# Values of three pairs loaded through GpSimd's casting queue, a last store on ScalarE's queue, zero matmuls in 16 places, and a new order of issue, in a gated recurrence with a two-layer feed-forward on one core

## The chip, the core and the metric

The kernel runs on one core of one Trainium2 chip. The time is device microseconds of one execution. The kernel before was timed five times: the median is 197.15 us, the lowest 194.38 us, the highest 199.48 us. One further execution was profiled; its own time was 197.51 us.

## The reference

There are 4 batches, 8 heads, 768 tokens and 48 numbers per head. For each batch and head a 48 x 48 state runs along the tokens, and its output goes through a two-layer network with the smooth activation 0.5 (h + sqrt(h^2 + 4)):

```
f = 1 / (1 + exp(-f_logit))
for t in range(768):
    state = f[t][:, None] * state + k[t][:, None] * v[t][None, :]
    y[t] = q[t] @ state
x = y as (4 * 768, 8 * 48)
h = x @ w_in                       # 384 x 2048
out = (0.5 * (h + sqrt(h * h + 4))) @ w_out   # 2048 x 384
```

All inputs and the output are float32 in device memory; the kernel multiplies in fp16 and accumulates in float32.

## The kernel before, in words

The tokens are cut into 12 pairs of chunks, 256 tokens each, three pairs to a batch. Token 2u+i of a pair lies on partition u, so that one partition's row of one head is two neighbouring tokens, 384 bytes in memory. Pair 0 is cut in two halves of four heads (FINE, line 18), the others are whole.

Each pair passes through these pieces, and their names are the words that the order is written in (the number after the name is the pair):

- lf, lk, lq, lv (lines 169 to 177): the loads of the gate, the keys, the queries and the values, 384 KB each, issued by SyncE.
- ex, ut, tt, ln, hi, lo (lines 179 to 268): the logarithm of the gates, split into two fp16 parts. ex and ln are ScalarE, ut is VectorE, the others can be on several engines.
- cu (line 272): TensorE sums the logarithms along the tokens. For pairs 0 to 2 it fills two banks, for the later ones one bank, and c1 (line 299) makes the second sum on VectorE.
- ep, ea (line 308) and ge (line 350): exponentials of the sums on ScalarE. gs and gb (lines 356 and 363) make decay factors of them.
- qu, ku (lines 320 and 326) and qm, km (line 333): queries and keys are scaled by the gates, into fp16 (the tile qk).
- vc (line 340): the values are cast to fp16 by a copy on VectorE, GpSimd or ScalarE.
- tp and te: for pairs 0 to 3 the scaled queries and keys are transposed by TensorE (line 381) and copied out (line 395). tx (line 371): for pairs 4 to 11 a transposing DMA issued by SyncE does it.
- sc (line 406) and pm (line 427): scores inside a chunk and their mask. kv (line 435): keys times values. sa, sb, sp, ia: the state is carried from chunk to chunk. yt and yn (lines 484 and 499): the output of the recurrence; yc (line 506) copies it out.
- xp and xe (lines 522 and 529), or for pairs 4 to 11 the transposing DMA xx (line 514): the output is transposed for the network.
- m1 (line 537): eight pieces of six matmuls for the first layer. sq (line 547) squares, rt (line 554) takes the root, gt (line 563) finishes the activation on VectorE. m2 (line 574): the second layer in two halves of four pieces. ev (line 585) copies the result out, st (line 595) stores it.
- wi and wo (lines 147 and 152): the weights, loaded and cast to fp16 by DMAs that GpSimd issues.

What runs when is one list, ORDER (lines 31 to 105), written ahead by a planner from the costs and the sets of reads and uses that stand beside each piece. A word is a name, a colon, the engine (D VectorE, P GpSimd, A ScalarE, S SyncE, T TensorE) and, for TensorE, an @ with the PSUM banks that the piece starts to use. The loop at line 685 emits the words in this order. So each engine has its own queue, in the order of its words in the list, and runs it strictly in turn; a word that waits for another engine holds up everything behind it on its own engine. A word that takes a buffer or a bank waits until the readers of what stood there are done (DEPTH, line 29, says how many buffers a name has; `os`, the tile that ev fills and st stores, has 2). TABLE:e and TABLE:s load one of two tables of functions into ScalarE.

The code already knows words that begin with wm (line 693): n matmuls of the identity into a bank that nothing reads. The order before uses none.

## Time and profile before

| what | us |
|---|---|
| median of five executions (lowest to highest) | 197.15 (194.38 to 199.48) |
| the profiled execution, its own time | 197.51 |
| its span, first to last instruction of the program | 195.3 |
| TensorE busy with matmuls in the span | 171.4 |
| VectorE, ScalarE, GpSimd busy | 151.5, 153.6, 117.5 |
| start of the first matmul | 6.45 |
| start of the first matmuls of the first layer (line 541) | 22.32 |
| end of the last matmul | 190.9 |
| start of the last two stores' issue on SyncE | 191.45 and 192.05 |

The profile's page gives busy time by engine, and the span in 40 slices of 4.9 us. The timeline gives instructions in order of time, those of one line merged, with the idle time of the engine before them and what ended it in brackets. The table of stretches gives, for any stretch, each engine's busy time, the clock that TensorE was granted, and what the DMA engines moved. PEld is the load of a stationary operand, which overlaps the matmuls. Times are from the span's start.

### The profile page before, as it was taken

The page shows a single profiled execution, that of the slowest core. Times are in us where ns is not written, and L with a number is a line of the kernel's source. Part 1 is how long each engine was busy: PE and PEld are TensorE (multiplying, and loading weights), DVE is VectorE, ACT ScalarE, POOL GpSimd, SP SyncE. Part 2 cuts the span into 40 slices and gives each one's busy share as a digit, 9 for nine tenths or more (in the row PEclk, how much of TensorE's full clock was granted, in tenths as well). Part 3 has the DMA queues.
Part 4 walks back from the last instruction along what each step waited for, and adds up shares of the span by engine and source line. Part 5 has one row for each costly group of instructions (what it writes and reads, how often), then busy time and mean ns, then how long its engine had stood idle before and what let it go on. Part 6 is the DMA issues. An engine that isn't in the chain of part 4 may idle for free.

```text
span 195.3 us, 5596 instructions
## 1 busy us (share of the span) xinstructions
PE 171.4 (88%) x2287; PEld 124.1 (64%) x2287; DVE 151.5 (78%) x280; ACT 153.6 (79%) x246; POOL 117.5 (60%) x146
## 2 busy tenths in 40 slices
PE   0348993789999999899999999999969999999990
...
PEclk9999999699999999999999999999999999999999
...
GB/s 142 268 256 236 245 219 248 213 237 226 223 242 121 226 251 136 263 215 228 209 230 206 230 145 229 169 189 53 31 153 147 51 85 82 3 0 0 164 68 93
DMA packets 80505, 32.87 MB, mean 168 GB/s; under 512 B 73824, under 2 KB 80480, under 8 KB 80480
## 3 DMA queue, kind: packets, MB, share of 16 engines
q1 hardware_dynamic: 76768, 29.37, 74.4%
q0 software_dynamic: 3712, 3.15, 10.0%
...
## 4 chain that ended last, share of the span: by engine, by line
PE 45%; POOL 23%; DMA 13%; issue 8%; DVE 5%; ACT 3%; SPq 1%; POOLq 0%; DVEq 0%
PE ps L541 19%; PE ps L578 19%; POOL qk L142 7%; DMA qkT<-qk 5%; DMA f<-in_f_logit_dram 3%; POOL k L142 3%; DMA k<-in_k_dram 3%; POOL UT L142 3%; DMA xT<-y 3%; DVE qk L142 2%; POOL v L139 2%; POOL q L142 2%; PE ps L414 2%; PE ps L492 2%; POOL hl L266 1%
## 5 line engine op out<-in xcount | busy, mean ns | idle before, releaser
L541 PE MATMUL ps<-xT,win 128*128 128x256 f16 x576 | 73.7, 276 | 3.2 <-ACT os L137 1.4
L566 DVE SCALAR_TENSOR_TENSOR g<-ps,r 128x512 f16<-128x512 f32 x96 | 62.4, 684 | 17.4 <-ACT r L556 17.2
L578 PE MATMUL ps<-wout,g 128*128 128x384 f16 x384 | 71.2, 327 | 0.0
L550 ACT ACTIVATE hsq<-ps 128x512 f16<-128x512 f32 x96 | 54.0, 592 | 16.4 <-PE ps L541 15.8
L541 PEld LDWEIGHTS <-win 128*128 128x128 f16 x576 | 55.3, 99 | 15.0 <-issue 2.3
L556 ACT ACTIVATE r<-hsq 128x1024 f16<-128x1024 f16 x48 | 50.6, 1057 | 1.2
L578 PEld LDWEIGHTS <-g 128*128 128x128 f16 x384 | 36.1, 98 | 19.5
L429 DVE TENSOR_TENSOR pm<-ps,mask 128x512 f16<-128x512 f32 x48 | 30.9, 683 | 3.8 <-PE ps L414 3.7
L142 POOL TENSOR_TENSOR qk<-q,ea 128x384 f16<-128x384 f32 x22 | 22.2, 1031 | 1.3 <-DVE q L142 0.9
L142 POOL TENSOR_TENSOR k<-k,UT 128x768 f32<-128x768 f32 x9 | 16.3, 1811 | 4.1 <-DMA k<-in_k_dram 4.1
L142 POOL TENSOR_TENSOR qk<-k,ep 128x384 f16<-128x384 f32 x18 | 17.6, 998 | 0.1
L283 PE MATMUL ps<-hl,tri 128*128 128x384 f16 (+1 forms) x34 | 9.2, 377 | 9.1 <-ACT hl L258 6.5
L181 ACT ACTIVATE f<-f 128x768 f32<-128x768 f32 (+1 forms) x13 | 10.3, 792 | 4.2 <-DMA f<-in_f_logit_dram 4.0
L139 POOL CAST v<-v 128x768 f16<-128x768 f32 (+1 forms) x11 | 9.0, 822 | 6.3 <-DMA v<-in_v_dram 6.3
L142 POOL TENSOR_TENSOR UT<-UT 128x384 f32<-128x384 f32 (+1 forms) x9 | 9.1, 1012 | 4.4 <-DVE UT L231 4.4
L137 ACT COPY os<-ps 128x384 f32<-128x384 f32 x9 | 4.3, 480 | 8.8 <-PE ps L578 5.0
L142 POOL TENSOR_TENSOR q<-q,UT 128x384 f32<-128x384 f32 x9 | 9.0, 996 | 3.8 <-DMA q<-in_q_dram 3.8
L414 PE MATMUL ps<-qkT 48*64 48x128 f16 x384 | 9.7, 228 | 1.5 <-ACT qkT L137 0.6
L266 POOL TENSOR_TENSOR hl<-s,hl 128x384 f16<-128x384 f32 (+1 forms) x11 | 10.1, 915 | 0.8 <-ACT hl L258 0.7
L414 PEld LDWEIGHTS <-qkT 48*64 48x64 f16 x384 | 6.7, 110 | 5.7 <-issue 3.2
L139 DVE CAST y<-ps 128x384 f16<-128x384 f32 x17 | 9.3, 550 | 0.9 <-PE ps L501 0.9
L139 DVE COPY os<-ps 128x384 f32<-128x384 f32 x15 | 8.2, 548 | 2.1 <-PE ps L578 2.1
...
## 6 DMA issues: line engine op xcount, KB each, us to landing
...
```

Source lines behind the costliest of these rows:

```text
L139: eng(e).tensor_copy(out=o, in_=i)
L142: eng(e).tensor_tensor(out=o, in0=a, in1=b, op=ALU.mult)
L181: nc.scalar.activation(out=t, in_=t, func=AF.Exp, scale=-1.0)
L266: eng(e).tensor_tensor(out=hl[:, 1, hs, 0:D], in0=T["s", p][:, hs], in1=hl[:, 0, hs, 0:D], op=ALU.subtract)
L283: nc.tensor.matmul(out=T["cum", p, m][:, h0 * D:h1 * D], lhsT=tri[:, m], rhs=t[:, hs, 0:D], start=(r == 0), stop=(r == len(terms) - 1), sk ...
L414: nc.tensor.matmul(out=T["sc", p, i, h][64 * cc:64 * cc + 64, j, :], lhsT=t[r, 1, j, i, :], rhs=t[r, 0, j], start=True, stop=True)
L429: eng(e).tensor_tensor(out=T["pm", p, i, h], in0=T["pc", p, i, h] if key in PMACT else T["sc", p, i, h], in1=K["mask"][:, i].unsqueeze(1). ...
L541: nc.tensor.matmul(out=T["h", p, m][:, a], lhsT=K["win"][m // 2][:, j, m % 2 * 256 + a * 128:m % 2 * 256 + a * 128 + 128], rhs=T["xT", p][ ...
L550: nc.scalar.activation(out=T["hsq", p, r][:, a], in_=T["h", p, m].rearrange("p a c t -> p (a c t)"), func=AF.Square, scale=1.0)
L556: nc.scalar.activation(out=T["r16", p, r], in_=T["hsq", p, r], func=AF.Sqrt, scale=0.25, bias=1.0)
L566: nc.vector.scalar_tensor_tensor(out=T["g", p][:, 2 * m:2 * m + 2, :].rearrange("p a t -> p (a t)"), in0=T["h", p, m].rearrange("p a c t - ...
L578: nc.tensor.matmul(out=T["o", p, cc], lhsT=T["g", p][:, jn, cc * 128:(cc + 1) * 128], rhs=K["wout"][jn // 4][:, jn % 4, :], start=(jn == 0 ...
```

## The change

- **Values by GpSimd's queue.** For pairs 1, 2 and 3 the words lv and vc go. In their place vd is a DMA issued by GpSimd that reads the float32 values and writes the fp16 tile. vd1 stands behind gs0 and between wi0 and qu1 in GpSimd's queue, vd2 behind gb1, after wi3 and before gs2, vd3 between qu4 and ku4.
- **One last store by ScalarE.** Of the four stores of pair 11, st11.1.1 is issued by ScalarE, directly behind ev11.1 in its queue, and st11.1.0 stays with SyncE.
- **Zero matmuls.** A tile of zeros, warm, is set by VectorE ahead of all other constants. Sixteen words wm3_n emit three matmuls of it each, 128 x 128: ten words between cu0.0 and tp0.0, one ahead of and one behind tp0.1, one ahead of m1.0.0, one behind m1.0.1, and two after the last m2. The number behind the underscore only makes the word unique.
- **The order.** The whole list is new. 39 words that stay change their engine between VectorE, GpSimd and ScalarE (qu2 from GpSimd to VectorE, km2 from VectorE to GpSimd, qm1 from GpSimd to VectorE, vc0.0 from GpSimd to ScalarE among them). The planner's cost of a store's issue by SyncE changes from 0.5 to 0.6.

The diff, with the list cut to what is spoken of:

```diff
@@ -27,81 +27,83 @@
+VDMA = [1, 2, 3]
...
-lf0.1:S lf0.0:S lf1.0:S lk0.0:S lk0.1:S TABLE:e ex0.1:A lq0.1:S ut0.1:D ex0.0:A lq0.0:S tt0.1:P ut0.0:D ln0.1:A tt0.0:D
-hi0.1:A ln0.0:A lf2.0:S lo0.1:P hi0.0:A ex1.0:A lo0.0:D lv0.0:S cu0.0:T@01 ku0.0:D ut1.0:D cu0.1:T@01 lk1.0:S ku0.1:D tt1.0:D
-ep0.1:A qu0.1:D ln1.0:A km0.1:D ea0.1:A ep0.0:A lq1.0:S qm0.1:D ea0.0:A hi1.0:A qu0.0:D tp0.1:T@12 lf3.0:S km0.0:D ex2.0:A
-qm0.0:D ge0:A te0.0.1:A ut2.0:D gs0:P lv0.1:S tp0.0:T@12 tt2.0:D lo1.0:P te0.0.0:A te0.1.0:D ln2.0:A lf4.0:S te0.1.1:D hi2.0:A
-ku1.0:D sc0.0:T@01 wi0:P sc0.1:T@23 cu1.0:T@45 wi2:P lv1.0:S qu1.0:D ex3.0:A pm0.01:D lk2.0:S lo2.0:P ea1.0:A pm0.10:D vc0.1:A
-vc0.0:P cu2.0:T@15 pm0.00:D lq2.0:S ge1:A qm1.0:P ep1.0:A pm0.11:D kv0:T@02 ge2:A ex4.0:A yt0:T@34 sa0:D km1.0:D yn0.1:T
-yc0.0:A gb1:P ia0.1:T yc0.1:A xp0.0:T@0 xe0.0:A xp0.1:T@3 ut3.0:D tp1.0:T@46 wi1:P xe0.1:A sb0:D ep2.0:A m1.0.1:T@0 tt3.0:P
-ea2.0:A te1.1.0:D m1.0.0:T@7 sq0.1:A wi3:P te1.0.0:D ln3.0:A lf5.0:S ut4.0:D sc1.0:T@12 gs1:P sq0.0:A sc1.1:T@34 pm1.00:D
-m1.0.4:T@5 TABLE:s rt0.0:A vc1.0:P pm1.11:D m1.0.5:T@1 tt4.0:P pm1.01:D kv1:T@46 gs2:P ia1.0:T pm1.10:D gb2:P hi3.0:P sq0.5:A
-lv2.0:S gt0.0:D yt1:T@23 ku2.0:P sq0.4:A yn1.0:T sa1:D m1.0.3:T@7 rt0.2:A yc1.0:D ia1.1:T m1.0.2:T@4 gt0.1:D sq0.3:A lo3.0:P
-yn1.1:T sb1:D xp1.0:T@0 sq0.2:A km2.0:D wo1:P rt0.1:A cu3.0:T@2 lk3.0:S m1.0.6:T@6 qu2.0:P yc1.1:D TABLE:e ln4.0:A c13.0:D
-xp1.1:T@3 lq4.0:S qm2.0:P xe1.1:D xe1.0:D m1.0.7:T@3 gt0.5:D ex5.0:A m1.1.1:T@0 gt0.2:D lq3.0:S ea3.0:A vc2.0:P gt0.4:D
-tp2.0:T@14 ge3:A sq0.7:A wo0:P ut5.0:D m1.1.3:T@5 sq1.1:A te2.1.0:D tt5.0:P sq0.6:A te2.0.0:D ep3.0:A wo2:P ln5.0:A lk4.0:S
...
-m2.7.00:T@0 gt7.5:D sq8.1:A st5.01.1:S m2.7.01:T gt7.6:D sq8.0:A tx10.1:S gs10:P m2.7.02:T gs11:P gt7.7:D rt8.0:A gb11:P
...
-m1.11.6:T@5 gt11.2:D m2.10.13:T sq11.6:A gt11.5:D m2.10.01:T sq11.7:A ev10.1:D m2.10.02:T rt11.3:A m2.11.01:T gt11.7:D
-m2.10.03:T gt11.6:D m2.11.02:T ev10.0:D m2.11.10:T@5 st10.01.1:S m2.11.11:T st10.01.0:S m2.11.03:T m2.11.12:T ev11.0:D
-m2.11.13:T st11.0.0:S st11.0.1:S ev11.1:A st11.1.0:S st11.1.1:S
...
+lf0.0:S lf0.1:S lf1.0:S lk0.0:S lk0.1:S TABLE:e ex0.0:A lq0.1:S ut0.0:D ex0.1:A lq0.0:S tt0.0:P ut0.1:D ln0.0:A tt0.1:D
+hi0.0:A ln0.1:A lf2.0:S lo0.0:P hi0.1:A ex1.0:A lo0.1:D lv0.0:S cu0.1:T@01 ku0.0:D ut1.0:D lk1.0:S cu0.0:T@01 ku0.1:D ep0.1:A
+wm3_42:T@2 km0.1:D ep0.0:A wm3_30:T@2 ea0.1:A qu0.1:D wm3_20:T@2 ea0.0:A wm3_38:T@2 qu0.0:D wm3_32:T@1 km0.0:D lf3.0:S lv0.1:S
+wm3_1:T@1 wm3_17:T@1 tt1.0:D ex2.0:A wm3_34:T@1 wm3_25:T@1 wm3_16:T@1 qm0.0:D ln1.0:A qm0.1:D tp0.0:T@12 vc0.0:A wm3_11:T@3
+ut2.0:D lq1.0:S tp0.1:T@12 hi1.0:A wm3_49:T@3 te0.0.0:A tt2.0:D lo1.0:P te0.1.1:A te0.0.1:D lf4.0:S te0.1.0:D ge0:A ln2.0:A
+wi0:P ku1.0:D sc0.0:T@01 lk2.0:S hi2.0:A sc0.1:T@23 cu1.0:T@45 vc0.1:A lo2.0:P pm0.01:D ex3.0:A lq2.0:S pm0.11:D gs0:P
+cu2.0:T@16 vd1.0:P ea1.0:A pm0.10:D ep1.0:A kv0:T@35 pm0.00:D ge1:A qu1.0:P lf5.0:S ea2.0:A sa0:D yt0:T@02 ep2.0:A wi2:P
+qm1.0:D ge2:A yn0.1:T yc0.0:A yc0.1:A wi1:P km1.0:D ex4.0:A xp0.1:T@0 xp0.0:T@1 wi3:P ia0.1:T xe0.1:A ut3.0:D tp1.0:T@23 gb1:P
+xe0.0:A ut4.0:D wm3_35:T@0 vd2.0:P te1.0.0:A m1.0.0:T@4 tt3.0:D m1.0.1:T@0 gs2:P te1.1.0:D ln3.0:A wm3_33:T@1 lk3.0:S sq0.0:A
+hi3.0:P sb0:D sc1.1:T@12 kv1:T@36 gs1:P sq0.1:A pm1.11:D ku2.0:P ia1.0:T TABLE:s rt0.0:A sc1.0:T@57 pm1.10:D pm1.01:D
+m1.0.4:T@1 km2.0:P pm1.00:D m1.0.5:T@2 sa1:D sq0.4:A yt1:T@57 gt0.1:D sq0.5:A yn1.0:T yn1.1:T gb2:P rt0.2:A yc1.0:D lo3.0:P
+m1.0.2:T@0 gt0.0:D lq3.0:S m1.0.3:T@3 sq0.2:A wo0:P qu2.0:D ia1.1:T xp1.0:T@4 sq0.3:A yc1.1:D cu3.0:T@5 qm2.0:P gt0.4:D
+rt0.1:A xp1.1:T@7 c13.0:D m1.0.7:T@1 xe1.0:D TABLE:e ea3.0:A tt4.0:P xe1.1:D gt0.2:D tp2.0:T@47 wo1:P sb1:D lq4.0:S ge3:A
+ex5.0:A te2.1.0:D kv2:T@06 wo2:P ia2.0:T ep3.0:A m1.0.6:T@7 ut5.0:D wo3:P sq0.7:A m1.1.0:T@5 sa2:D tt5.0:P ln4.0:A te2.0.0:D
...
+yc9.0:D m1.7.6:T@0 rt8.0:A yc9.1:D gs10:P m1.8.5:T@2 tx10.0:S sp10.0:D sq7.6:A m1.7.7:T@6 vc11.0:D sa10:P tx10.1:S m1.8.6:T@4
+sq7.7:A gt8.0:D m1.8.3:T@7 rt7.3:A gt8.1:D st6.01.1:S km11.0:P m1.8.7:T@1 st5.01.1:S sq8.6:A gt7.6:D m2.7.10:T@3 xx9:S sq8.7:A
+sp10.1:D gt8.6:D m2.7.00:T@6 sq8.3:A tx11.1:S gt8.5:D m2.7.01:T ev7.1:A sc10.0:T@45 gt8.4:D sq8.2:A sc10.1:T@23 st6.01.0:S
...
+m1.10.7:T@6 sq10.5:A m1.10.6:T@5 gt10.0:D sq10.7:A m2.9.00:T@1 gt10.1:D sq10.6:A m1.11.0:T@4 sq10.4:A m2.9.01:T rt10.3:A
+m2.9.02:T rt10.2:A gt10.7:D m1.11.1:T@2 m1.11.5:T@6 sq11.0:A gt10.5:D m2.9.03:T sq11.5:A gt10.6:D m1.11.4:T@7 sq11.1:A
+gt10.2:D m1.11.6:T@5 gt10.4:D rt11.0:A m1.11.2:T@3 m2.10.10:T@0 sq11.4:A gt11.0:D m2.10.11:T rt11.2:A gt11.1:D m2.10.00:T@4
+ev9.0:D m1.11.3:T@2 gt11.4:D st9.01.0:S m1.11.7:T@1 st8.01.1:S sq11.3:A m2.11.00:T@7 st9.01.1:S sq11.6:A m2.10.01:T st8.01.0:S
+sq11.2:A rt11.1:A m2.10.12:T m2.10.13:T sq11.7:A gt11.2:D m2.10.02:T rt11.3:A gt11.3:D m2.10.03:T gt11.5:D m2.11.10:T@2
+ev10.1:A gt11.6:D m2.11.01:T ev10.0:D m2.11.02:T gt11.7:D st10.01.0:S m2.11.11:T st10.01.1:S m2.11.03:T m2.11.12:T ev11.0:D
+m2.11.13:T st11.0.0:S wm3_13:T@0 st11.0.1:S wm3_26:T@0 ev11.1:A st11.1.1:A st11.1.0:S
...
@@ -166,7 +168,7 @@
         for x, (h0, h1) in enumerate(parts):
             hs = slice(h0, h1)
             nh = h1 - h0
-            for s in "fqkv":
+            for s in ("fqk" if p in VDMA else "fqkv"):
                 def load(e, bk, s=s, x=x, hs=hs, p=p):
                     if (s, p) not in T:
                         T[s, p] = sb(s, p, [128, 8, 2, 48], FP32)
@@ -337,12 +339,21 @@
                     W.add(f"{nm}m{p}.{x}", "DP", qm, reads=[f"{nm}u{p}.{x}", f"{en}{p}.{x}"], makes=[f"{nm}g{p}.{x}"],
                           uses=[(nm, p), (en, p), ("qk", p)], lock=True, cost={"D": 0.18 + 1.15e-3 * 2 * n, "P": 0.2 + 2.3e-3 * 2 * n})
 
-            def vc(e, bk, x=x, hs=hs, p=p):
-                if ("v16", p) not in T:
-                    T["v16", p] = sb("v16", p, [128, 8, 2, 48], FP16)
-                copy(e, T["v16", p][:, hs], T["v", p][:, hs])
-            W.add(f"vc{p}.{x}", "DPA", vc, reads=[f"v{p}.{x}"], makes=[f"vv{p}.{x}"], uses=[("v", p), ("v16", p)],
-                  lock=True, cost={"D": 0.07 + 0.94e-3 * 2 * n, "P": 0.19 + 0.84e-3 * 2 * n, "A": 0.2 + 0.85e-3 * 2 * n})
+            if p in VDMA:
+                def vd(e, bk, x=x, hs=hs, p=p):
+                    if ("v16", p) not in T:
+                        T["v16", p] = sb("v16", p, [128, 8, 2, 48], FP16)
+                    bb, t0 = divmod(p * 256, 768)
+                    nc.gpsimd.dma_start(out=T["v16", p][:, hs].rearrange("p h i d -> p h (i d)"),
+                                        in_=v[bb][hs, t0:t0 + 256, :].rearrange("h (p i) d -> p h (i d)", i=2))
+                W.add(f"vd{p}.{x}", "P", vd, makes=[f"vv{p}.{x}"], uses=[("v16", p)], dma=("w", 1.55 * nh / 8), cost={"P": 1.1})
+            else:
+                def vc(e, bk, x=x, hs=hs, p=p):
+                    if ("v16", p) not in T:
+                        T["v16", p] = sb("v16", p, [128, 8, 2, 48], FP16)
+                    copy(e, T["v16", p][:, hs], T["v", p][:, hs])
+                W.add(f"vc{p}.{x}", "DPA", vc, reads=[f"v{p}.{x}"], makes=[f"vv{p}.{x}"], uses=[("v", p), ("v16", p)],
+                      lock=True, cost={"D": 0.07 + 0.94e-3 * 2 * n, "P": 0.19 + 0.84e-3 * 2 * n, "A": 0.2 + 0.85e-3 * 2 * n})
 
         def allx(nm, p=p, xs=xs):
             return [f"{nm}{p}.{x}" for x in xs]
@@ -597,8 +608,8 @@
                     t0 = p * 256 + c * 128
                     eng(e).dma_start(out=out[t0:t0 + 128 * n, :].rearrange("(c u i) d -> i u c d", c=n, i=2)[i],
                                      in_=T["os", p][64 * i:64 * i + 64, c:c + n])
-                W.add(f"st{p}.{''.join(map(str, cs))}.{i}", "SP" if p in SPLIT_OUT else "S", st, reads=[f"os{p}.{c}" for c in cs], makes=[],
-                      uses=[("os", p)], dma=("o", 0.28 * len(cs)), cost={"S": 0.5, "P": 0.8})
+                W.add(f"st{p}.{''.join(map(str, cs))}.{i}", "SPA" if p in SPLIT_OUT else "S", st, reads=[f"os{p}.{c}" for c in cs], makes=[],
+                      uses=[("os", p)], dma=("o", 0.28 * len(cs)), cost={"S": 0.6, "P": 0.8, "A": 0.6})
 
 
 @with_exitstack
@@ -620,6 +631,8 @@
     psp = ctx.enter_context(tc.tile_pool(name="psp", bufs=1, space=PSUM))
     D = 48
 
+    warm = konst.tile([128, 128], FP16, name="warm")
+    nc.vector.memset(warm, 0.0)
     tri2 = konst.tile([128, 2, 64], FP16, name="tri2")
     nc.gpsimd.memset(tri2, 0.0)
     for c in range(2):
@@ -692,8 +705,8 @@
             e, _, banks = rest.partition("@")
             if name.startswith("wm"):
                 t = ps(banks, [128, 128], FP32)
-                for n in range(int(name[2:])):
-                    nc.tensor.matmul(out=t, lhsT=ident, rhs=ident, start=True, stop=True)
+                for n in range(int(name[2:].split("_")[0])):
+                    nc.tensor.matmul(out=t, lhsT=warm, rhs=warm, start=True, stop=True)
                 continue
             W.pieces[name].emit(e or W.pieces[name].eng, banks)
 
```

## The prediction

> **What bounds the kernel now.** First the page: its row of slices, the clock, and the two kinds of DMA queue.
>
> ```profile
> PE   0348993789999999899999999999969999999990
> ...
> PEclk9999999699999999999999999999999999999999
> ...
> q1 hardware_dynamic: 76768, 29.37, 74.4%
> q0 software_dynamic: 3712, 3.15, 10.0%
> ```
>
> From slice 8 (39 us) on TensorE is full but for slice 29. So time is to be won in the head, in that slice, and behind the last matmul. A packet of SyncE's queue takes 0.744 x 195.3 x 16 / 76768 = 30 ns of an engine, one of GpSimd's 84 ns. The table of stretches prices the holes (columns: length, busy PE, PEld, DVE, ACT, POOL, clock, DMA share, GB/s):
>
> ```profile
> 30.00:35.00 5.00, 1.45 (x18) 1.00 (x18) 3.84 (x4) 3.67 (x5) 4.90 (x5) 0.99 0.97 237
> 35.00:40.00 5.00, 4.20 (x52) 2.70 (x49) 4.08 (x9) 2.84 (x7) 4.44 (x7) 0.66 1.17 234
> ...
> 140.00:145.00 5.00, 3.65 (x72) 2.57 (x70) 3.24 (x6) 1.13 (x3) 4.33 (x8) 1.00 1.10 132
> ```
>
> TensorE idles 3.5 us at 30 to 35; then (1 - 0.66) x 5 / 0.5 = 3.4 us run at half clock. TensorE's timeline shows the waits, and the clock's price: twelve matmuls of line 541 in 2.72 us instead of 1.48.
>
> ```profile
> 32.05 0.32 PE L283 MATMUL ps<-hl,tri 128*128 128x384 f16 x1 [2.10 <-POOL hl L266]
> ...
> 34.73 0.35 PE L525 MATMUL ps<-ident,y 128*128 128x128 f16 x3 [1.51 <-DVE y L139]
> 35.53 2.72 PE L541 MATMUL ps<-xT,win 128*128 128x256 f16 x12 [0.45 <-DVE xT L139]
> ...
> 43.51 1.48 PE L541 MATMUL ps<-xT,win 128*128 128x256 f16 x12
> ```
>
> GpSimd's timeline shows what is behind both waits:
>
> ```profile
> 29.32 1.80 POOL L142 TENSOR_TENSOR k<-k,UT 128x768 f32<-128x768 f32 x1 [2.06 <-DMA k<-in_k_dram]
> 31.09 0.90 POOL L266 TENSOR_TENSOR hl<-s,hl 128x384 f16<-128x384 f32 x1
> ```
>
> The keys of pair 2 (lk2) were issued at 15.25 and landed at 29.3. ku2 waits for them, lo3 (which cu3 needs) and, on VectorE, km2 queue behind ku2, and yc1.1 behind km2 (31.16 to 34.2). So until 39 us the bound is the order of transfers; after that TensorE's own work.
>
> **What the Trainium skill says.** "DMA: Bandwidth & Descriptors", Queues, rings and completion order: each DMA engine goes round between its queues, a packet at a time. The trace agrees: before the weights flow, loads land 1.4 us apart (k1 13.30, q1 14.72, f3 16.17); beside them v1 lands at 24.64, k2 at 29.26, q2 at 31.43. Same page, SWDGE vs HWDGE vs iDMA: a cast is GpSimd's alone, whose cores compute a descriptor pair for each piece moved. Here 384 and 512 pieces cost 0.83 and 0.79 us of GpSimd; no run shows 1024. "TensorE: Matmul & The Clock Gate", Part 1: half clock until a window of about 3.4 us has been busy, and the window runs freely. The half-clock stretch of 3.4 us agrees; before about 21 us durations are those of a slow clock too (sc0 1.07 us, sc1 0.64).
>
> **The change part by part, head first.** The loads up to f2 are unmoved, so ex2 starts at 11.26 as now. ScalarE then runs ex2 0.84, ln1 0.53, vc0.0 0.50, hi1 0.52 to 13.65. VectorE has the same work up to the last qm0 (12.4); its extra memset of warm (0.17, the row of L632) fits into the 0.53 us before ut0. tp0.0 and tp0.1 run from 11.8 to 13.4 with three zero matmuls between. Four te follow, two per engine (0.58 each on ScalarE), and sc0 starts at 14.85: 0.9 later than now.
>
> **Zero matmuls.** At the skill's 107 ns each when slow, three take 0.32 us. Ten words are 3.2 us from 8.2, the end of cu0, to 11.4, where TensorE waits for VectorE until 11.8: hidden. Later cover would cost 0.3 a word; the four others near tp0 and m1.0 cost 0.3 to 1.0 where TensorE is partly idle. The two last stand behind the last m2: nothing. If the clock rises before sc0, then sc0, cu1, cu2, kv0 and yt0 save 0.4 + 0.6 + 0.6 + 0.3 + 0.3 = 2.2 us of TensorE, though not all on the path; bound below by nothing. I take half a gain: cu2 now waits for bank 5 (0.52 idle) and takes bank 6 instead, so yt0 ends at about 19 to 20.5 (now 20.2). ScalarE's ex4 stands ahead of xe0, so m1.0 starts at 22.5 (now 22.32). No gain so far.
>
> **Values by GpSimd.** GpSimd: lo1 to 14.6, wi0 to 15.4, lo2 (hi2 at 16.05) to 17.0, gs0 to 17.3, vd1 0.8 to 1.1 (a DMA's 0.83 below; in proportion to 1024 pieces 2.2 above; I take 1.1), qu1, wi2, wi1, wi3, gb1, vd2 to 23.1, gs2, hi3, gs1 to 24.7. Two casts of 0.82 go from GpSimd and one of 0.88 from ScalarE, so three issues cost GpSimd about 1.7 us more in all. SyncE's queue loses three loads. Behind f4 k2 comes at once, in the place where v1 landed, 24.6; q2 one place later, about 29. ku2 runs 24.7 to 26.5, km2 (now GpSimd's, 2 x 0.99) to 28.5, gb2, lo3, wo0 (0.2 + 0.9 + 0.8) to 30.4, qm2 to 32.5. So tp2 starts at 32.6 instead of 38.2. But in the new order m1.0.6 and m1.1.1 (2 x 0.65) stand behind it: the gain in useful work is 5.6 - 1.3 = 4.3 us. What is late next: q2, on VectorE's qu2, with yc1.1 behind it; and v1 for kv1. I take off 0.8 for these and a slow window: **3.5**.
>
> A packet of vd (384 bytes in, 192 out) I price as a load's, 30 ns: 1024 x 30 / 16 = 1.9 us, and v1, behind wi0 in the queue, lands at about 24 to 25, where kv1 wants it (now 25.70). The upper bound is the weights' 84 ns: 5.4 us.
>
> vd3 costs 1.1 us of GpSimd while that is 4.1 to 4.7 us busy of 5 (45 to 60 us); it hides as long as TensorE has m2 to do, and costs up to 1.1 where not. kv3 comes late enough not to see v3.
>
> **The middle.** The view of waits has what makes slice 29:
>
> ```profile
> ACT os L137 <- DMA out_dram<-os: 3.9, 1, 3.9
> ...
> PE ps L541 <- ACT os L137: 1.4, 1, 1.4
> ```
>
> At 140 to 144 us ScalarE's ev7 waits for a store of os that SyncE issues behind tx10's wait for its own input, and a matmul waits for the bank that ev7 frees. The new list still has that store behind both tx10, but sc10 stands 5.3 us of TensorE's work further back (2.4 of it the head's zero matmuls), and ev7.1 close to it. I take **0.5** of the 1.5 lost; from -1.5 (new waits of this sort) to +1.5.
>
> **The end.** The last two issues by SyncE start at 191.45 and 192.05 and land at 193.62 and 194.25. On ScalarE the last starts with the first: **0.6**; to nothing, if ScalarE's own issue is slow at first. But m1.11.7 stands 13 pieces of m2 before the end where its counterpart stood 11. Behind it are four sq, two rt (4 x 0.59 + 2 x 1.06 = 4.5) and four gt and an ev, to 6.9 us, and m2.11.03 comes after ten pieces, 6.5: **-0.4**.
>
> Sum: 3.5 + 0.5 + 0.6 - 0.4 = 4.2, so the span of 195.3 becomes 191.1; with the 2.2 us around it (197.51 - 195.3) 193.3. The profiled execution is 0.36 above the median of the runs shown, so I predict **193.0 us** against 197.15. A measurement of this kernel tells about 2% (3.9 us) from no change.
>
> **Rivals.**
>
> - The head's gain is given back: between 40 and 60 us ScalarE, VectorE and GpSimd are each busy 4 to 5 of every 5 us, and a different list puts waits of half a microsecond in many places. Against it: TensorE, with m2 in reserve, was full there. 195 to 197.5.
> - Slower: vd's packets cost as the weights' do. Then v1 lands at 18.4 + 2 + 5.4, stretched by half beside the loads, about 28.5; TensorE, in order, stands at kv1 for 4 us, its clock falls again, and k2 and q2 lose the same DMA time in front of ku2. That takes the 4.3 and adds 2 to 4: 198 to 202. It decides from about 60 ns a packet. For it: all of GpSimd's packets seen were dear. Against: they read 2 KB, these 384 bytes.
> - The zero matmuls do not raise the clock, since after them TensorE has little to do until 14.85: the forecast plus 0.5 to 1.5, 193.5 to 195.
> - More is won: clock up before sc0 and no stall at sc10: 188.5 to 190.5.
>
> **How the numbers follow.** Forecast (190.5 to 195) 0.42, given back 0.22, clock not raised 0.08, slower by the packets 0.18, more won 0.10. The range of 189 to 200 leaves out some 0.05 below and 0.13 above. Faster by over 2% (below 193.2): 0.32 of the forecast and the 0.10, 0.42. Slower by over 2% (above 201.1): part of the packets' case and mishaps in the list, 0.17. Within 2%: 0.41.
>
> **What would show it.** Right: vd issues near 1 us; v1 landed by 25, k2 by 25; tp2 before 34; no idle of over 2 us between 25 and 35 and no half clock after 22; the last two stores landing together. Wrong: kv1 waiting for a DMA, full clock only from 21 us or lost again later, holes at sc or ev that slice 29 shows now.

## The result, and the profile after

The kernel after takes 197.59 us (median; 194.78 to 199.69); the kernel before, run beside it, 197.52 us (193.63 to 202.25). Execution against execution the ratio is 1.0088, with a 95% interval of 1.0056 to 1.0121: 0.9% slower, less than the 2% that count as a difference here. (The ratio is over the undisturbed executions of each kernel, so it isn't the quotient of the medians: of 169 executions of the kernel before that ran beside the experiments, the 70 that were granted at least 0.994 of TensorE's clock took 194.7 us in the median and the 99 others 198.2, and the execution that the prediction read, with 0.991, is one of the slower kind.) The forecast was 193.0 us; the rival "given back" had 195 to 197.5, so the result lies just above that. The profiled execution took 198.13 us, with a span of 196.2.

The page of the kernel after, the rows that were shown of before:

```profile
PE   0698879699999997999999998999999999999992
...
PEclk9999999879999999999999999999999999999998
...
q1 hardware_dynamic: 73568, 28.09, 70.5%
q0 software_dynamic: 6832, 3.74, 13.5%
```

(The clock's row, like the clock's column in the tables of stretches, shows full clock up to the first recorded rise, at 21.10 us here, only because nothing is recorded before it: the zero matmuls ahead of the rise start 0.107 us apart, those behind a rise, in e15, 0.055.) TensorE is busier in slices 1 and 2 (the zero matmuls), the hole of slice 29 is gone, and there is a new one in slice 15 (73.6 to 78.5 us). GpSimd's queue has 3120 packets more in 3.5% more of the engines' time; of 16 x 196.2 us against 16 x 195.3 that is (0.135 x 3139 - 0.100 x 3125) / 3120 = 36 ns for a packet of vd. So they aren't dear: the rival that decided from 60 ns falls.

The same three stretches as before:

```profile
30.00:35.00 5.00, 4.67 (x80) 3.51 (x78) 3.85 (x10) 4.46 (x7) 4.31 (x7) 1.00 1.34 208
35.00:40.00 5.00, 3.42 (x61) 2.48 (x61) 4.14 (x9) 4.51 (x9) 4.98 (x7) 0.82 1.25 238
140.00:145.00 5.00, 5.00 (x90) 4.48 (x89) 3.95 (x8) 4.31 (x7) 4.20 (x6) 1.00 0.40 59
```

The idle 3.5 us at 30 to 35 are gone and so is the hole at 140. But 35 to 40 is emptier than before (3.42 us of work for 4.20), and has half clock again. TensorE's timeline says why:

```profile
28.89 1.49 PE L552 MATMUL ps<-xT,win 128*128 128x256 f16 x12 [1.34 <-DMA win<-in_moe_w_in_dram]
...
34.93 0.78 PE L401 MATMUL ps<-ident,qk 64*128 64x64 f16 x32
37.29 0.52 PE L453 MATMUL ps<-v,qk 64*128 64x96 f16 x16 [1.58 <-DMA v<-in_v_dram]
...
37.91 2.51 PE L552 MATMUL ps<-xT,win 128*128 128x256 f16 x12
```

The first line is m1.0.4, which waits for a weight; the second is tp2; the third is kv2, which waits for the values of pair 2, now a load of GpSimd; the fourth is the price of the half clock that follows (2.51 us for 1.48). GpSimd's timeline, from which the two waits come:

```profile
18.12 0.94 POOL L347 DMA_DIRECT2D v<-in_v_dram  x1
...
20.03 2.34 POOL L150 DMA_DIRECT2D win<-in_moe_w_in_dram  x3
...
22.89 0.91 POOL L347 DMA_DIRECT2D v<-in_v_dram  x1
...
26.58 1.80 POOL L144 TENSOR_TENSOR k<-k,UT 128x768 f32<-128x768 f32 x1
...
30.53 0.92 POOL L268 TENSOR_TENSOR hl<-s,hl 128x384 f16<-128x384 f32 x1
```

The last two lines are ku2, 2.7 us earlier than before, and lo3, which is only 0.6 us earlier, since km2, now GpSimd's, stands between them. ku2's keys had been there since 22.5; it came 4.1 us later because hi3, ahead of it on GpSimd, waited for ScalarE:

```profile
25.93 0.50 POOL L141 CAST hl<-s 128x384 f16<-128x384 f32 x1 [1.57 <-ACT s L250]
```

vd1, three weights and vd2 are issued within 5.7 us, but they land one behind the other: 26.3, then 28.8, 31.5, 34.1, then 37.2. Before, the weights landed at 24.1, 27.6 and 30.9 and v2, by SyncE, at 34.2.

A second new wait is ScalarE's, at 73 us, for the gates of pair 8:

```profile
75.79 0.84 ACT L183 ACTIVATE f<-f 128x768 f32<-128x768 f32 x1 [2.65 <-DMA f<-in_f_logit_dram]
```

and SyncE's timeline shows the load behind a transpose that itself waits for GpSimd:

```profile
66.98 2.29 SPq L384 DMA_TRANSPOSE qkT<-qk  x1
69.32 0.57 SPq L176 DMA_DIRECT2D f<-in_f_logit_dram  x1
```

**Where the time went.** TensorE's useful matmuls (the zero ones left out) can be added up in the order of the list, at their length at full clock, about 160 us in all; the table gives the time at which each kernel has done so much of them. It is worked out from the traces.

| useful TensorE work, us | before | after | difference |
|---|---|---|---|
| 2 | 14.99 | 17.44 | +2.45 |
| 13 | 33.21 | 34.23 | +1.02 |
| 15 | 38.30 | 38.25 | -0.05 |
| 20 | 44.76 | 45.32 | +0.56 |
| 45 | 70.46 | 71.69 | +1.23 |
| 60 | 87.09 | 89.31 | +2.22 |
| 110 | 139.36 | 142.39 | +3.03 |
| 115 | 146.26 | 147.42 | +1.16 |
| 158 | 189.70 | 190.76 | +1.06 |
| span | 195.29 | 196.17 | +0.87 |

The head ends 0.6 behind instead of 3.5 ahead; the middle loses 2.5 more; the old hole, once gone, gives 1.9 back; the tail gives 0.2.

### The profile page after: what moved, and what is told of

It is laid out like the page before. It is cut to its first block, busy times and chain, and to the rows that moved or that the text cites. A ratio compares the mean times of both kernels' runs of the same rounds, so it can differ in the third digit from the quotient of the medians.

```text
span 196.2 us, 5685 instructions
## 1 busy us (share of the span) xinstructions
PE 176.7 (90%) x2335; PEld 128.6 (66%) x2335; DVE 151.9 (77%) x282; ACT 155.4 (79%) x249; POOL 113.5 (58%) x142
## 4 chain that ended last, share of the span: by engine, by line
PE 55%; POOL 15%; DMA 14%; issue 6%; DVE 5%; ACT 3%; SPq 0%; POOLq 0%
PE ps L589 22%; PE ps L552 21%; DMA v<-in_v_dram 7%; POOL qk L144 6%; DMA f<-in_f_logit_dram 5%; PE ps L709 3%; PE ps L425 2%; DMA xT<-y 2%; PE ps L453 2%; POOL hl L268 2%; PE ps L503 2%; PE ps L512 2%; PE ps L285 1%; POOL win L150 1%; DVE g L577 1%
## 5 line engine op out<-in xcount | busy, mean ns | idle before, releaser
L552 PE MATMUL ps<-xT,win 128*128 128x256 f16 x576 | 72.8, 275 | 1.9 <-DMA win<-in_moe_w_in_dram 1.6
L561 ACT ACTIVATE hsq<-ps 128x512 f16<-128x512 f32 x96 | 54.9, 594 | 18.2 <-PE ps L552 17.3
L144 POOL TENSOR_TENSOR qk<-q,ea 128x384 f16<-128x384 f32 x20 | 19.9, 1013 | 2.3 <-DVE q L144 1.2
L144 POOL TENSOR_TENSOR qk<-k,ep 128x384 f16<-128x384 f32 x20 | 19.9, 1016 | 1.7 <-ACT ep L314 1.5
L233 DVE TENSOR_SCALAR UT<-f 128x768 f32<-128x768 f32 (+1 forms) x13 | 7.7, 604 | 4.6 <-ACT f L183 4.4
L144 POOL TENSOR_TENSOR UT<-UT 128x384 f32<-128x384 f32 (+1 forms) x8 | 7.8, 978 | 5.7 <-DVE UT L233 5.7
L141 DVE COPY os<-ps 128x384 f32<-128x384 f32 x14 | 7.6, 551 | 3.3 <-PE ps L589 3.1
L144 POOL TENSOR_TENSOR q<-q,UT 128x384 f32<-128x384 f32 x8 | 8.0, 1000 | 3.3 <-DMA q<-in_q_dram 3.2
L285 PEld LDWEIGHTS <-tri 128*128 128x128 f16 x34 | 3.2, 110 | 7.9 <-DVE tri L667 3.8
```

The lines of the kernel that those rows point to most:

```text
L141: eng(e).tensor_copy(out=o, in_=i)
L144: eng(e).tensor_tensor(out=o, in0=a, in1=b, op=ALU.mult)
L285: nc.tensor.matmul(out=T["cum", p, m][:, h0 * D:h1 * D], lhsT=tri[:, m], rhs=t[:, hs, 0:D], start=(r == 0), stop=(r == len(terms) - 1), sk ...
L552: nc.tensor.matmul(out=T["h", p, m][:, a], lhsT=K["win"][m // 2][:, j, m % 2 * 256 + a * 128:m % 2 * 256 + a * 128 + 128], rhs=T["xT", p][ ...
L561: nc.scalar.activation(out=T["hsq", p, r][:, a], in_=T["h", p, m].rearrange("p a c t -> p (a c t)"), func=AF.Square, scale=1.0)
```

## Experiments

All times are medians in us; the ratio is to the kernel before, run beside each. Rows without a ratio are single executions; e4 and e5 have four each, e8 six, the others 14 to 22.

| run | edit | us | ratio, 95% interval |
|---|---|---|---|
| e1_no_zeros | after, no zero matmuls | 195.33 | 1.0015, 0.9984 to 1.0046 |
| e2_wide_zeros | after, each word one 128 x 512 of zeros | 196.42 | |
| e3_same_ones | after, triangles of ones in their place | 197.64 | |
| e12_wide_data | after, each word one 128 x 512 of real numbers | 195.26 | |
| e14_long_warm | e12 and nine of ones from 1.5 us on | 194.53 | |
| e15_one_word | after, ten words in one | 196.01 | 1.0014, 0.9968 to 1.0060 |
| e4_vd2_early | after, vd2 behind vd1 | 199.21 | 1.0150, 0.9963 to 1.0336 |
| e5_vd_alone | before, with vd1 to vd3 | 198.77 | 1.0176, 1.0065 to 1.0286 |
| e6_lf8_first | after, lf8 ahead of tx5.1 | 196.11 | 1.0045, 1.0004 to 1.0085 |
| e7_store_alone | before, last store by ScalarE | 193.52 | |
| e8_mended | after, edits of e1, e4 and e6 | 198.92 | 1.0218, 1.0139 to 1.0297 |
| e9_plain_lf8 | after, edits of e1 and e6 | 195.97 | 1.0054, 1.0023 to 1.0086 |
| e10_v2_back | e9, v of pair 2 by SyncE | 195.11 | 0.9981, 0.9946 to 1.0015 |
| e11_all_v_back | e9, v of all pairs by SyncE | 195.81 | 0.9984, 0.9934 to 1.0033 |
| e13_sync_queue | e10, three moves in SyncE's queue | 193.97 | 0.9913, 0.9874 to 0.9951 |
| e16_early_zeros | e13, zeros in two unbroken words | 194.16 | 0.9938, 0.9903 to 0.9973 |

### The zero matmuls: what they cost, and why the clock didn't rise

**Without them.**

```diff
-wm3_42:T@2 wm3_30:T@2 wm3_20:T@2 wm3_38:T@2 wm3_32:T@1
...
-wm3_13:T@0 wm3_26:T@0
```

> The changed kernel without the sixteen zero-matmul words. Theory: the ten words between cu0.0 and tp0.0 held tp0.0 back to 13.2 us (30 matmuls of 170 ns) and never raised the clock. Without them tp0.0 starts near 11.8 us, sc0.0 near 14.5 instead of 16.0, and the clock still turns full near 21 us, as in both kernels so far; kv0 and m1.0.0 come 1 to 1.5 us earlier; kv2 still waits for v of pair 2 until about 37 us, so the end gains 0 to 1 us. Rival (the words do raise the clock early or hold it): full clock comes a window of 3.4 us later, at 24 to 25 us, or the half clock at 38 lasts longer, and the time rises by 1 us or more.

Its ratio is 0.7% below that of after, the intervals apart. sc0 starts at 14.50 (after: 16.03), and full clock comes at 19.38. So the zero matmuls cost time and gave none.

**Wider, or other numbers.** Two runs of one execution each.

```diff
-warm = konst.tile([128, 128], FP16, name="warm")
+warm = konst.tile([128, 512], FP16, name="warm")
...
-for n in range(int(name[2:].split("_")[0])):
-    nc.tensor.matmul(out=t, lhsT=warm, rhs=warm, start=True, stop=True)
+for n in range(1):
+    nc.tensor.matmul(out=t, lhsT=warm[:, 0:128], rhs=warm, start=True, stop=True)
```

> The changed kernel with each zero-matmul word as one matmul of 512 columns of zeros instead of three of 128, which is about the same time (10 x 0.43 us) with a third of the weight loads. Theory A: the clock asks for a large share of columns streamed in its window, and three matmuls of 128 in 0.53 us are only 384 columns of some 640 that fit. Then dense columns, zeros or not, bring full clock one or two windows earlier than 21.1 us, at 14.3 or 17.7. Theory B: zeros do not count as work: full clock at 21.1 us as before.

Ten wide ones took 6.18 us, and full clock came only at 27.17; why later than in the other runs isn't shown.

```diff
-nc.tensor.matmul(out=t, lhsT=warm, rhs=warm, start=True, stop=True)
+nc.tensor.matmul(out=t, lhsT=tri[:, 0], rhs=tri[:, 1], start=True, stop=True)
```

> The changed kernel with the same sixteen words of three matmuls of 128 columns, but the operands are the triangles of ones (the tile tri) instead of zeros. Theory A (share of columns): full clock stays at 21.1 us. Theory B (zeros do not count): full clock one or two windows of 3.4 us earlier, at 14.3 or 17.7 us.

Thirty took 5.12 us, as the zeros did, and full clock came at 19.63. Neither width nor these numbers helped. A third run put width and real numbers together (the tile and the one matmul a word as in the wide zeros):

```diff
-nc.tensor.matmul(out=t, lhsT=warm, rhs=warm, start=True, stop=True)
+nc.tensor.matmul(out=t, lhsT=tri[:, 0], rhs=hl[0].rearrange("p s h d -> p (s h d)")[:, 0:512], start=True, stop=True)
```

> As the kernel after, with each word of three zero matmuls replaced by one matmul of 128 x 512 on the logarithms of the gates (the operands of cu0), into a bank that nothing reads: the same density as the run with wide zeros, with real numbers. Theory A (the clock asks for switching numbers, not for busy time): full clock at the end of the first window that falls within the ten words, before 18 us, and sc0 and cu1 at full clock. Theory B (a run of 6 us is too short against the freely running window, whatever the numbers): no full clock before 19.5 us, as in every run so far. The time itself should be 195 to 199.

Ten took 6.18 us from 7.94, with a whole clock window inside them (8.29 to 11.70: the recorded stretches of half clock are 3.413 us long, and this window is three such steps ahead of the recorded rise at 21.94). The clock still rose only at 21.94:

```profile
8.29:11.70 3.41, 3.13 (x7) 0.65 (x6) 3.31 (x10) 0.97 (x5) 0.00 (x0) 1.00 1.04 255
```

So it isn't the numbers, and theory A of this run fell. Theory B's reason, too short a stretch, wasn't right either, as the next run shows, which adds a word to this one.

```diff
-lv0.0:S cu0.1:T@01
+lv0.0:S wm9_1:T@2 cu0.1:T@01
...
-nc.vector.memset(warm, 0.0)
+nc.vector.memset(warm, 1.0)
...
-for n in range(1):
-    nc.tensor.matmul(out=t, lhsT=tri[:, 0], rhs=hl[0].rearrange("p s h d -> p (s h d)")[:, 0:512], start=True, stop=True)
+for n in range(9 if name.startswith("wm9") else 1):
+    nc.tensor.matmul(out=t, lhsT=warm[:, 0:128] if name.startswith("wm9") else tri[:, 0], rhs=warm if name.startswith("wm9") else hl[0].rearrange("p s h d -> p (s h d)")[:, 0:512], start=True, stop=True)
```

> As the run with wide matmuls of real numbers, with nine more 128 x 512 matmuls of ones ahead of cu0.1, from about 1 us on, so that TensorE is busy without a gap from about 1 us to about 14 us. Ten wide ones alone, with a whole window of 3.4 us inside them, did not raise the clock, and the earliest rise in any run came at 18.3. Theory A (the clock needs several busy windows, or a longer history): full clock before 16 us. Theory B (before about 18 us it does not rise whatever TensorE does): sc0 and the first cu1 still at half clock, full clock between 17.5 and 22.

The clock was full from 5.80 us, so one window was enough: theory A had the time right, but not its reason. TensorE's timeline has the nine and, further on, most of sc0 at full speed:

```profile
1.46 4.02 PE L709 MATMUL ps<-warm 128*128 128x512 f16 x9 [1.46 <-DVE warm L635]
...
14.38 0.64 PE L425 MATMUL ps<-qkT 48*64 48x128 f16 x31 [0.16 <-DVE qkT L141]
```

The nine took 0.446 us each, where the wide ones of the two runs above took 0.618. The nine stand in one word; the others are words of one each, in the same bank as the word ahead. So the suspect is what stands between two words. (So theory A of the wide zeros, a large share of streamed columns, wasn't put to the test by them: of a wide word's 0.618 us an unbroken matmul needs 0.446.)

**In one word.** In the trace of after, two matmuls of a word start 0.107 us apart. A word in the same bank as the word ahead starts its first matmul 0.367 us behind that word's last, its second 0.060 and its third 0.107 later: 0.534 us a word, where three times 0.107 is 0.321. Where the bank changes (once, from 2 to 1) the next word starts 0.107 us on, as inside a word. This fits a wait of each word, as a new user of the bank, until the matmul before it has ended; the page counts it as busy. Eight of the ten words have it: 30 x 0.107 + 8 x 0.213 = 4.9 us, and the last matmul's own length makes it the 5.12 us measured.

```diff
-wm3_42:T@2 wm3_30:T@2 wm3_20:T@2 wm3_38:T@2 wm3_32:T@1 wm3_1:T@1 wm3_17:T@1 wm3_34:T@1 wm3_25:T@1 wm3_16:T@1
+wm30_42:T@2
```

> The kernel after, with the ten words of three zero matmuls between cu0 and tp0 put together into one word of thirty at the place of the first; the other six words stay. In the trace of after, two matmuls of a word start 0.107 us apart, but a word that takes the same bank as the word ahead of it starts 0.367 us behind that word's last matmul, and TensorE counts as busy meanwhile. Theory (the words wait for their own bank: eight such waits of 0.21 us make the ten words 5.1 us long): thirty in one word take 3.2 to 3.5 us, end near 11.4, tp0 starts at about 11.8 and sc0 near 14.5 as without zero matmuls, and the time is 0.4 to 0.7 per cent under the kernel after. The clock rises before 15 us only if a window of 3.4 us falls almost wholly into the stretch from 7.3 to 11.4. Rival (a zero matmul itself costs 170 ns): 5.1 us again and no change.

After's timeline of TensorE, with the ten words, tp0.0 and sc0:

```profile
8.03 5.12 PE L709 MATMUL ps<-warm 128*128 128x128 f16 x30
13.21 0.61 PE L401 MATMUL ps<-ident,qk 64*128 64x64 f16 x16
...
16.03 1.44 PE L425 MATMUL ps<-qkT 48*64 48x128 f16 x32 [0.81 <-ACT ge L363]
```

The same of the run with one word:

```profile
8.27 3.41 PE L709 MATMUL ps<-warm 128*128 128x128 f16 x30
11.61 0.51 PE L401 MATMUL ps<-ident,qk 64*128 64x64 f16 x16
...
14.56 0.64 PE L425 MATMUL ps<-qkT 48*64 48x128 f16 x31 [0.17 <-DVE qkT L141]
```

Thirty zero matmuls in 3.41 us, tp0.0 at 11.61, and in this execution the clock rose at 11.70, at the end of a window (8.29 to 11.70) that the word filled: zeros do raise it when they run without breaks. Where the window falls isn't the reason: in e6 below, which has the ten words as after has them, a window in nearly the same place lies wholly inside them (7.87 to 12.98), and the clock rose three windows later, at 22.14:

```profile
8.49:11.90 3.41, 3.13 (x21) 2.16 (x21) 3.31 (x11) 1.26 (x5) 0.00 (x0) 1.00 1.26 262
```

Two stretches of the run with one word, each one window of the clock, show what it takes to keep it:

```profile
8.29:11.70 3.41, 3.41 (x33) 3.21 (x31) 3.31 (x12) 1.69 (x5) 0.00 (x0) 1.00 1.28 262
11.70:15.11 3.41, 2.07 (x70) 1.48 (x70) 2.94 (x7) 3.36 (x9) 1.79 (x2) 1.00 1.29 261
```

The second, with TensorE busy for 2.07 of 3.41 us in small transposes and scores, lost it again at 15.11, so that cu1 and cu2 ran at half clock all the same. The ratio is that of the run without any zero matmuls (1.0014 and 1.0015): within its interval, about 0.5% to either side, they now cost nothing and win nothing. The rival, a dear zero matmul, falls.

**Is an early clock worth anything?** In the best of the kernels below (e13) I put zero matmuls into TensorE's idle time ahead of cu0, without breaks.

```diff
-lv0.0:S cu0.1:T@01
+lv0.0:S wm11_1:T@2 cu0.1:T@01
...
-cu0.0:T@01
+cu0.0:T@01 wm6_1:T@3
```

Each matmul is 128 x 512.

> As the kernel with SyncE's queue mended (no zero matmuls of the change, lf8 first, v of pair 2 on SyncE, lv4 and two stores moved), with zero matmuls put in without breaks: one word of eleven 128 x 512 ahead of cu0.1, where TensorE has nothing to do from about 1.5 to 6.4 us, and one word of six behind cu0.0. Ones in that place, with ten more words behind cu0, raised the clock at 5.8 us. Theory on the clock (it rises at the end of a window that is busy without breaks, zeros or not): full clock at some time between 5 and 9 us in most executions, sc0 at 0.64 us instead of 1.44. Rival (zeros do not count as work): first full clock at 18 to 22 us as before. On the time: kv1 waits for v of pair 1 to about 24.4 and m1.0 for a weight to about 27 whatever TensorE does before, so I expect within 0.5 per cent of the same kernel without them, faster by at most 1 us.

The clock was full from 4.20 to 14.44 in the profiled execution, then half until 24.68. So sc0, from 14.53, still took 1.45 us, and the ratio, 0.9938 and no better than e13's 0.9913, doesn't price a clock that stays. In e14, where full clock lasted from 5.80 through all of cu2, yt0 started at 17.65 us instead of the 21.11 of after, and then TensorE waited 1.76 us for v1 at kv1 (24.68) and 1.73 us for a weight (27.54). In this one execution TensorE is idle for what it has won, since v1 and the weights come when the DMA engines bring them.

### The values by GpSimd

**vd2 earlier.** If kv2's wait for v2 were simply a load issued too late, an earlier one would cure it.

```diff
-wi0:P
...
-vd1.0:P
...
-gb1:P xe0.0:A ut4.0:D wm3_35:T@0 vd2.0:P
+vd1.0:P vd2.0:P
...
+gb1:P xe0.0:A ut4.0:D wm3_35:T@0
```

> The changed kernel with vd2 moved in GpSimd's queue from behind wi3 to directly behind vd1, nothing else. Theory: v of pair 2 landed at 37.2 us because it stood behind three weight loads in GpSimd's DMA queue; now it lands before 31, kv2 does not wait (1.6 us) and the clock does not fall at 38 (1.5 us), while win1 and win3 land about 1.4 us later, which m1.0.2 and others may wait for. At kv2 the kernel is 1 to 3 us earlier than the changed kernel; at the end 0.5 to 2.5 us faster. Rival (the middle's own waits decide, the head is absorbed): kv2 earlier, but the end within 0.5 us.

v2 landed at 29.4 instead of 37.2, but the weights behind it at 32.0, 34.7 and 37.3, and m1.0.4 waited the longer:

```profile
32.01 2.74 PE L552 MATMUL ps<-xT,win 128*128 128x256 f16 x12 [4.58 <-DMA win<-in_moe_w_in_dram]
```

The cure fell; it moves the lateness from v2 to the weights, three times the 1.34 us of after. A run with two other mends added, no wm words and lf8 behind lf9, went the same way (m1.0.4 at 30.82 after a wait of 4.79):

```diff
-vd1.0:P
+vd1.0:P vd2.0:P
...
-lf9.0:S
+lf9.0:S lf8.0:S
```

> The changed kernel with three edits together: no zero matmuls, vd2 directly behind vd1, lf8 ahead of tx5.1. Theory: the three losses are separate and add: 2 to 5 us faster than the changed kernel, and 1 to 4 us faster than the kernel before. Rival: TensorE's own work from 45 us on and new waits absorb them, and it is within 1 us of the kernel before.

**The values alone,** in the kernel before:

```diff
-lv1.0:S lv2.0:S lv3.0:S vc1.0:P vc2.0:P vc3.0:A
...
-wi0:P
+wi0:P vd1.0:P
...
-wi3:P
+wi3:P vd2.0:P
...
-wo3:P
+wo3:P vd3.0:P
```

> The kernel before with v of pairs 1 to 3 through GpSimd's casting queue and nothing else: lv1 to lv3 and vc1 to vc3 go, vd1 stands behind wi0, vd2 behind wi3, vd3 behind wo3. Theory: k of pair 2 lands near 23 us instead of 29.3, ku2 no longer waits 2.1 us, tp2 starts 2 to 3 us earlier than 38.2, the half clock at 35 us goes or moves; the end is 1 to 3 us faster. Rival: the values become the late ones (kv1 or kv2 waits for a DMA) and the end is the same or slower.

k2 landed at 24.4 as forecast (before: 29.3) and tp2 came at 36.95 instead of 38.19, but TensorE waited 2.81 us for a weight that it doesn't wait for in the kernel before, and the whole was 1.8% slower (four executions):

```profile
27.95 1.49 PE L551 MATMUL ps<-xT,win 128*128 128x256 f16 x12 [2.81 <-DMA win<-in_moe_w_in_dram]
```

So the values alone, by this route, don't pay in the old order either. The weight isn't the whole of it: at 15 us of useful work this execution is still about 1 us ahead of the profiled one of the kernel before, and it keeps full clock from 22.72 on; it falls behind between 40 and 45, where TensorE waits 1.42 us at 67.39 for the transposing DMA of pair 4, which landed at 67.3 (before: 65.2).

**v of pair 2 back, then all of them,** in the new order with the two mends of e1 and e6. First that kernel itself, without the wm words:

```diff
-lf9.0:S
+lf9.0:S lf8.0:S
...
-cu7.0:T@0 lf8.0:S
+cu7.0:T@0
```

> The kernel after without its sixteen words of zero matmuls and with lf8 moved from behind tx5.1 to directly behind lf9 on SyncE; the three value loads by GpSimd stay where they are. The two edits alone gave 0.7 and 0.4 per cent. Theory (the costs are separate: 1.4 us of zero matmuls in the head, 2 us of waiting for f8 in the middle): they add, 193.8 to 195 us, about 1.1 to 1.5 per cent under the kernel after and level with the kernel before or just under it. Rival (one cover: what the head wins is waited for again at the next late transfer): no better than the better of the two, 195.3 to 196.2.

Its ratio is no better than that of either edit alone (1.0015, 1.0045): the rival was right. At 50 us of useful work it is where the two others are or ahead (75.26; e1 76.26, e6 76.16), at 60 it isn't (87.79; 87.92, 87.17). In the head it still has kv2's wait and the half clock behind it:

```profile
35.62 0.82 PE L453 MATMUL ps<-v,qk 64*128 64x96 f16 x16 [1.51 <-DMA v<-in_v_dram]
...
36.67 2.52 PE L552 MATMUL ps<-xT,win 128*128 128x256 f16 x12
```

Now v of pair 2 by SyncE:

```diff
-VDMA = [1, 2, 3]
+VDMA = [1, 3]
...
-lq2.0:S
+lq2.0:S lv2.0:S
...
-vd2.0:P
...
-qm2.0:P
+qm2.0:P vc2.0:P
```

> As the kernel with no zero matmuls and lf8 first, and the values of pair 2 go back to SyncE and a cast: lv2 behind lq2 and ahead of lf5, the cast vc2 on GpSimd behind qm2, where kv2 wants it. Theory (v of pair 2 is late because it stands behind three weight loads in GpSimd's DMA queue, and kv2's wait of 1.6 us brings the half clock): kv2 no longer waits for a DMA, no half clock near 36 to 42, 1.5 to 3 us less than the same kernel with vd2, about 192 to 193. Rival (the DMA engines are the limit up to 37 us whichever queue asks): f5 and k3 or a weight become late by the same 2 us instead, and the time stays within 0.5 us of the kernel with vd2.

v2 landed at 32.9, kv2's wait for a DMA is gone, and there is no half clock after 19.3 in this execution:

```profile
34.72 0.50 PE L453 MATMUL ps<-v,qk 64*128 64x96 f16 x15 [0.25 <-DVE sn L144]
...
35.33 0.82 PE L552 MATMUL ps<-xT,win 128*128 128x256 f16 x6
```

The ratio falls by 0.7%, intervals apart, about the least that was expected; f5 is 0.2 us later and k3 is not. So v2's late landing was the cause of that part, and where v2 stood in its queue the cause of the landing. How much of it is kv2's wait and how much the half clock isn't told apart.

```diff
-VDMA = [1, 2, 3]
+VDMA = []
...
-lf4.0:S
+lf4.0:S lv1.0:S
...
-lq2.0:S
+lq2.0:S lv2.0:S
...
-lq4.0:S
+lq4.0:S lv3.0:S
...
-gb1:P
+gb1:P vc1.0:P
...
-qm2.0:P
+qm2.0:P vc2.0:P
...
-qm3.0:P
+qm3.0:P vc3.0:P
```

The vd words are taken out.

> As the kernel with no zero matmuls and lf8 first, and the values of all three pairs go back to SyncE and casts: lv1 behind lf4, lv2 behind lq2, lv3 behind lq4; the casts on GpSimd behind gb1, qm2 and qm3. So of the change only the order and the last store by ScalarE are left. Theory (the loads by GpSimd cost by themselves, since the kernel before with them alone was 1.8 per cent slower): 191.5 to 194, faster than the kernel before. Rival (the new order needs k2 early, which only the values by GpSimd give): k2 lands at 27 to 28 again, tp2 starts near 37, and the time is 195 or more.

0.9984, the same as with v of pairs 1 and 3 by GpSimd; the theory's 191.5 to 194 us didn't come. k2 landed at 24.8, not at 27, and tp2 started at 33.78 (e9 33.34, before 38.19): the rival's reason fell, though the time is the one it named. The new order brings early keys and an early tp2 without the values' route. It also issues the weights later: without any value load by GpSimd three of them land at 26.0, 28.4 and 31.9 (before 24.1, 27.6 and 30.9), with vd1 ahead of them, in e9, at 27.2, 29.9 and 32.5. What is left of the change here, the order and the last store, with lf8's move, wins nothing measurable against the kernel before.

### SyncE's queue in the middle

**lf8 ahead of tx5.1.**

```diff
-lf9.0:S
+lf9.0:S lf8.0:S
...
-cu7.0:T@0 lf8.0:S
+cu7.0:T@0
```

> The changed kernel with lf8 moved in SyncE's queue from behind tx5.1 to ahead of it (directly behind lf9). Theory: ScalarE's 2.65 us wait for f of pair 8 at 73 to 76 us, and with it TensorE's 1.45 us wait for sc5.0 at 77 us, come from lf8 being issued behind the transpose tx5.1, which itself waits for km5; both go, tx5.1 may come some 0.6 us later, and the kernel is 1 to 2 us ahead of the changed one at 80 us and at the end. Rival: another wait takes its place at once (the transpose or GpSimd's chain), and the end is within 0.5 us.

The wait of 2.65 us is gone: from 45 to 50 us of useful work it takes 5.30 us (70.86 to 76.16) where after takes 6.98. With it goes 0.4% of the time, the intervals of the two ratios overlapping. The wait is not in every execution: in the traces of e1, e2 and e12, which issue lf8 where after does, ScalarE waits for f8 0.31 us, not at all, and 0.51 us, and TensorE not at all at sc5.0. There f8 landed 4.1 to 4.3 us after its issue, in after 6.5.

**Three more moves.** In e10 the same is seen twice more: v of pair 4 was issued behind both tx4 and landed at 67.5, and the stores of pair 0 stand behind both tx5. SyncE's timeline of e10:

```profile
66.11 4.21 SPq L384 DMA_TRANSPOSE qkT<-qk  x2
70.42 2.55 SPq L609 DMA_DIRECT2D out_dram<-os  x2
```

and VectorE's, where a copy waits for the buffer that these stores empty:

```profile
75.37 0.56 DVE L141 COPY os<-ps 128x384 f32<-128x384 f32 x1 [2.26 <-DMA out_dram<-os]
```

The edit moves all three ahead:

```diff
-tx4.0:S
+lv4.0:S tx4.0:S
...
-tx5.1:S
+st0.01.1:S st0.01.0:S tx5.1:S
```

The three words are taken out where they stood.

> As the kernel with no zero matmuls, lf8 first and v of pair 2 back on SyncE, with two more moves in SyncE's queue alone: lv4 directly ahead of tx4.0 (it was behind both tx4 and landed at 67.5), and the stores of pair 0, st0.01.1 and st0.01.0, directly ahead of tx5.1 (they were behind both tx5, were issued at 70.4 and held a copy of VectorE for 2.26 us). That kernel was 1.5 us ahead of the one with lf8 first at 40 us of useful TensorE work and level with it at 60. Theory (what the head wins is lost again at 60 to 85 us because SyncE's queue, in strict order, holds loads and stores behind transposes that wait for GpSimd): the lead stays, the span becomes 191 to 192, 0.4 to 0.8 per cent less. Rival (VectorE and GpSimd are themselves full from 60 to 70 us and set the pace there): no change of over 0.5 us.

The copy waits no more:

```profile
75.29 0.54 DVE L141 COPY os<-ps 128x384 f32<-128x384 f32 x1
```

v4 landed at 59.9. Between 40 and 60 us of useful work this execution took 20.84 us, that of e10 23.30. The ratio is 0.7% below e10's, the intervals just touching (0.9951 and 0.9946), 0.9% below the kernel before and 1.7% below the kernel after (0.9913 / 1.0088): the lowest of all. The rival, full engines, fell as far as the trace shows. Which of the moves does most wasn't tried.

### The last store

```diff
-st11.1.1:S
+st11.1.1:A
```

> The kernel before with its last store st11.1.1 issued by ScalarE and nothing else. Theory: the stretch from the end of the last matmul to the end of the span shrinks by 0.2 us or less, as between the two kernels (4.4 to 4.2 us), because the other store of the pair still waits its turn behind st11.0 on SyncE's queue or the two share the DMA engines. Rival: the whole issue of 0.6 us is saved.

From the end of the last matmul to that of the span it is 4.07 us instead of 4.4: a gain of 0.3. What this execution shows beside the edit matters more. Its head is that of the kernel before, word for word, and yet cu3 waited only

```profile
30.67 0.32 PE L283 MATMUL ps<-hl,tri 128*128 128x384 f16 x1 [0.42 <-POOL hl L266]
```

instead of 2.10: k2 landed at 27.9, not at 29.3, the clock didn't fall until the last matmul was done, tp2 started at 34.40 and 15 us of useful work were done at 34.52, not at 38.30. Whether the hole at 32 us costs 4 us or next to nothing differs between executions of one and the same head.

## Why the prediction was wrong, step by step

**What bounds the kernel.** The chain was read rightly: k2, ku2, lo3, cu3, then half clock. But its size came from one execution, and e7 shows the same words almost without it: tp2 at 34.40 there, by no edit to the head, is ahead of the 34.93 of after. In such an execution most of the 4.3 us was not there to be won.

**Values by GpSimd** is the step that failed, in its sentence "What is late next". Its prices held: vd issues of 0.94 and 0.91 us (I had 1.1), 36 ns a packet (30), v1 at 26.3 (24 to 25), k2 at 22.5 (24.6). It named q2 and v1 as next. I left out what stands behind vd1 in its own queue, the weights wi2, wi1 and wi3, and v2, which the change puts behind them, and never asked when kv2 wants it. v2 came 3 us later than before, the weights 3 to 5 us. The weights' part isn't vd1's alone: the new order issues the first of the three at 17.95 instead of 15.09 and has them 0.8 to 1.9 us late without any value load (e11), with vd1 ahead they are 0.6 to 1.5 later (e9), and with the zero matmuls another 0.7 (after against e1). These are single executions; e1 and e9, whose heads are alike, differ by 0.9 themselves. tp2 gained 3.3 us (34.93; I had 32.6), and then kv2's 1.58 and the half clock behind it, with the 1.34 of m1.0.4 ahead of it, took everything: level at 15 us of useful work. By the ratios v2's place cost 0.7% (e9 against e10) and the zero matmuls 0.7% (after against e1); with both mended, and lf8, the kernel is level with the one before and not 2% ahead. The Trainium skill's "DMA: Bandwidth & Descriptors", Queues, rings and completion order, has each DMA engine go round between the queues that have work for it. I used it for what SyncE's queue gets beside GpSimd's and not for the other side: a load that leaves SyncE's queue stands in GpSimd's instead, and in the trace v1, three weights and v2 land in the order of issue, v2 13.4 us after its issue was done. And the early keys that this was to pay for come with the new order alone (e11).

**Zero matmuls** are the second step that failed: I called them hidden. "107 ns each when slow" is right within a word and the sum is wrong: 5.12 us instead of 3.2, since a word waits for the matmul before it in the same bank, 0.213 us for eight of ten. The Trainium skill's "TensorE: Matmul & The Clock Gate", Single matmul latency, has a constant of some 183 ns between a slow matmul's start and its end beyond its columns. Inside a word the trace doesn't show it (0.107 us from start to start); between two words it shows 0.213, within 30 ns of it. That put tp0 at 13.21 instead of 11.8 and sc0 at 16.03 (14.50 in e1), m1.0 at 24.38 where I had 22.5, and ku2 at 26.58 (24.96 in e1) where I had 24.7. The half of 2.2 us for an early clock wasn't there: words broken by waits didn't raise it. Part 1 of that page, a window that has been busy, fits the unbroken words (e14, e15, e16); the others fit it only if the waits between words don't count, though the profile's page has them as busy.

**The middle.** The gap of slice 29 closed as argued, for 1.9 us instead of 0.5. The allowance for new waits was -1.5; they took 2.5 in this execution, the largest the one for f8 behind tx5.1 (1.7 us against e6; the traces of e1, e2 and e12 don't show it). I had read the new list for stores behind tx10, the place that hurt before, and not for loads behind tx5.

**The end.** 0.6 for the store was 0.2 (after) to 0.3 (e7); the -0.4 of the chain behind m1.11.7 didn't show (the last 43 us of work took 43.44 and 43.34).

**The rivals.** "Given back" was nearest, but by other means than half-microsecond waits. Dear packets: refuted (36 ns). "The zero matmuls do not raise the clock": true for the change, and dearer than I had it. In sum, of the four terms +3.5, +0.5, +0.6 and -0.4, the first came out as -0.6, the second as -0.6 (1.9 less 2.5), the two others as +0.2 and +0.1: 0.9 us lost where 4.2 were to be won.

**Still open:** why the values alone cost 1.8% in the old order (0.7 to 2.9% by its interval, from four executions) and no more than 0.7% in the new one (e9 against e11, intervals overlapping).
